# Moving the value products of three attention chunks, spreading weight traffic and adding one output buffer in a fused attention and feed-forward kernel

## The chip, the cores and the metric

The kernel runs on one core of one Trainium2 chip. The metric is the time of one execution on the device in microseconds (us). The core's engines are TensorE (PE, with its weight loads shown apart as PEld), VectorE (DVE), ScalarE (ACT), GpSimd (POOL) and SyncE (SP), which here issues nearly all the DMA transfers. Each engine runs its own instructions in order and waits for the others at semaphores.

## The reference

Eight batches, eight heads, 576 positions, head size 64, in float32. Heads 0 to 3 see a plain window of 32 positions, heads 4 to 7 every fourth position of a window of 128. The attention's output goes through a feed-forward network with an exact gelu.

```python
scores = scale * np.matmul(q, k.transpose(0, 1, 3, 2))
rel = pos[:, None] - pos[None, :]
mask_plain = (rel >= 0) & (rel < window)
mask_dil = (rel >= 0) & (rel < window * dilation) & (rel % dilation == 0)
...
attn = attn / (np.sum(attn, axis=-1, keepdims=True) + 1e-09)
return np.matmul(attn, v).astype(np.float32)
...
x = np.ascontiguousarray(attn_out.transpose(0, 2, 1, 3)).reshape(B * S, H * D)
h = x @ w_in
g = 0.5 * h * (1.0 + erf(h * inv_sqrt2))
return (g @ w_out).astype(np.float32)
```

x is 4608 tokens by 512, w_in 512 by 2048, w_out 2048 by 512.

## The kernel before

**Tiles.** The 4608 tokens are nine chunks of 512: chunks 0 to 7 are the first 512 positions of the eight batches, chunk 8, the last, holds the remaining 64 positions of all of them. Inside a chunk the attention works on four pairs of heads, two plain and two dilated, as blocks of queries against blocks of keys: score products, mask, exp, sums, norm, a transposition, and the *value products* (attention times v), each called a visit here. The feed-forward network works with float32 values split into a high and a low part, and each product is the three products of parts that matter.

**Stage 1, chunk 0 and the attention of chunks 0 and 1.** The order is written out by hand in the string `SCHEDULE`. Each job is a Python generator; a token such as `half0.1.1:a` advances one job by a step on a named engine (a for ACT, d for DVE). The order of the tokens is the order of the instructions on every engine, SP's DMA issues among them. `av0.0` and the like are the value products: `av_wide` (L488) for chunk 0, with v read at 128 rows, `av_early` (L500) for chunk 1. `norm`, `turn` and `half` make what they read: `turn0.3` transposes on TensorE, `half0.x.y` copies it into place. The weights come in as 64-bit words and are split on DVE and ACT (`split`, `rest`, `high`, `join`); `keep0` and so on store a finished weight tile of 1 MB to DRAM (`keep_weight`, L648).

**Stage 2, chunks 1 and 2.** Plain feed-forward: 12 products L603 for a block f of the hidden layer, gelu, then 12 products L626 into the output. Other work is put between by `add(position, rank, job)`: a position counts units of 12 products, with 32 units for each of the two parts of a chunk (positions 32 to 96), and everything due by a position is emitted when the unit is reached. Such work is the attention of later chunks (`whole(2, ...)`, `whole(3, ...)`, `whole(4, ...)`: their scores, softmax, key swaps L379, value products `av_four`, L571, and `x_back`, which give the chunk's x), storing weight tiles 8 to 15, reloading tiles 0 to 7 (`fetch_weight`, L764), and sums of weight tiles (`prepare`) with their stores (`keep_sums`, L804).

**Stage 3, pairs of chunks.** Chunks (3, 4), (5, 6) and (8, 7) go in pairs by seven products of sums in place of eight. A unit of position is one product of 6 multiplications (L1028); a quarter q has 28 products, four quarters a pair. Weights and weight sums come through a ring of tiles from DRAM (`ring_load`, L983). `combine` makes the operands from the chunks' x (L907 on ACT, L912 on DVE), `first_layer` makes the gelu's operands (ACT L1049 stashes a bank in a buffer named u, L1053 copies a bank, L1058 the gelu, L1074 and L1075 the high and low part), `drains` (L1081) adds results from the banks into accumulators on DVE (L1090). The attention of later chunks runs between; for the last chunk's dilated heads (`L23`) the value products are `av_last` (L519) and ACT's copies `x_wide` (L586).

**Buffers.** The pool tag "go" has three buffers, shared in turn by the identity `eye`, the gelu's output `gf`, the output tile `o_sb` before its store, and `u`. A tile takes a buffer when the third tile before it is done with.

## Time and profile before

| | us |
|---|---|
| median of three runs | 890.93 (890.57 to 891.88) |
| profiled execution | 889.42 |
| its span | 887.56 |

The profile shows one execution. Busy time of an engine is the time in which one of its instructions runs; TensorE's mean granted clock over the span is 0.969 of full speed. A row of a timeline joins like instructions that follow each other; the bracket at its end holds the idle time of the engine before them and what ended it. "issue" is idle time in which the engine waited for nothing that the profile shows. A float32 product that isn't split shows as two loads and two products in the trace, so its counts are doubled.

### The profile page before, as it was taken

The page shows a single profiled execution, that of the slowest core. Times are in us where ns is not written, and L with a number is a line of the kernel's source. Part 1 is how long each engine was busy: PE and PEld are TensorE (multiplying, and loading weights), DVE is VectorE, ACT ScalarE, POOL GpSimd, SP SyncE. Part 2 cuts the span into 40 slices and gives each one's busy share as a digit, 9 for nine tenths or more (in the row PEclk, how much of TensorE's full clock was granted, in tenths as well). Part 3 has the DMA queues.
Part 4 walks back from the last instruction along what each step waited for, and adds up shares of the span by engine and source line. Part 5 has one row for each costly group of instructions (what it writes and reads, how often), then busy time and mean ns, then how long its engine had stood idle before and what let it go on. Part 6 is the DMA issues. An engine that isn't in the chain of part 4 may idle for free.

```text
span 887.6 us, 19932 instructions
## 1 busy us (share of the span) xinstructions
PE 827.9 (93%) x8400; PEld 674.6 (76%) x8400; DVE 613.3 (69%) x703; ACT 464.5 (52%) x1081; POOL 95.4 (11%) x92
## 2 busy tenths in 40 slices
PE   7899889998997999899999998997989999999997
PEld 5787768886885877688888876885768777888885
DVE  8697762346675379485959798856538798483977
ACT  7587633543765356473645663744546545243351
POOL 1000002042202430000000026000000045000000
PEclk9999979999998999999999998998899999999999
DMA  9996494932689836877768685966356668566663
GB/s 365 415 419 227 137 421 183 386 104 103 223 313 363 309 125 236 315 246 226 274 202 297 191 310 168 318 225 215 103 165 232 198 205 260 174 205 191 197 198 126
DMA packets 118296, 212.31 MB, mean 239 GB/s; under 512 B 6848, under 2 KB 92864, under 8 KB 110784
## 3 DMA queue, kind: packets, MB, share of 16 engines
q1 hardware_dynamic: 118064, 210.79, 68.1%
q8 instruction: 66, 1.08, 0.5%
q10 hardware_dynamic: 144, 0.26, 0.1%
q14 instruction: 22, 0.18, 0.1%
HBM read 161.21 MB, written 42.99 MB: 230 GB/s over the span
## 4 chain that ended last, share of the span: by engine, by line
PE 77%; DVE 12%; issue 5%; ACT 3%; DMA 2%; SPq 0%; DVEq 0%; ACTq 0%
PE ps L1028 43%; PE ps L603 15%; PE ps L626 13%; PE ps L303 2%; DVE g L1075 2%; PE ps L571 2%; DVE xc L912 2%; DMA raw_w<-w 2%; DVE acc L1090 1%; ACT xn L592 1%; DVE xn L920 1%; DMA outT<-o_sb 1%; PE ps L497 1%; DVE xn L584 1%; PE ps L515 1%
## 5 line engine op out<-in xcount | busy, mean ns | idle before, releaser
L1028 PE MATMUL ps<-xc,ring 128*128 128x512 f32 x1008 | 240.1, 397 | 4.6 <-ACT ps L1053 4.0
L1028 PE MATMUL ps<-g,ring 128*128 128x512 f32 x1008 | 237.4, 395 | 5.5 <-DVE g L1075 2.7
L1028 PEld LDWEIGHTS ps<-g,ring 128*128 128x128 f32 x1008 | 191.2, 191 | 49.4 <-DVE g L1075 5.5
L1028 PEld LDWEIGHTS ps<-xc,ring 128*128 128x128 f32 x1008 | 191.0, 191 | 47.4 <-ACT ps L1053 4.2
L1075 DVE TENSOR_TENSOR g<-g_value,g 128x1024 fp32r<-128x1024 f32 x84 | 103.5, 1241 | 78.9 <-ACT g L1074 78.9
L603 PE MATMUL ps<-x,weight 128*128 128x512 f32 x576 | 142.7, 403 | 1.6 <-issue 1.6
L626 PE MATMUL ps<-g,weight 128*128 128x512 f32 x576 | 136.3, 394 | 1.5 <-issue 1.5
L603 PEld LDWEIGHTS ps<-x,weight 128*128 128x128 f32 x576 | 110.3, 194 | 26.3 <-issue 2.2
L626 PEld LDWEIGHTS ps<-g,weight 128*128 128x128 f32 x576 | 109.3, 190 | 23.3 <-issue 0.2
L1074 ACT CAST g<-g_value 128x1024 fp32r<-128x1024 f32 x84 | 87.1, 1046 | 38.4 <-DVE g_value L1076 21.6
L615 DVE TENSOR_TENSOR g<-gf,g 128x512 fp32r<-128x512 f32 x48 | 35.7, 744 | 76.0 <-ACT g L105 75.9
L1090 DVE TENSOR_TENSOR acc<-ps,acc 128x1024 f32<-128x1024 f32 x56 | 67.6, 1217 | 28.7 <-PE ps L1028 28.7
L1104 POOL TENSOR_TENSOR acc<-acc 128x1024 f32<-128x1024 f32 x14 | 42.1, 3018 | 370.8 <-DVE acc L1090 370.4
L610 ACT ACTIVATE gf<-ps 128x512 f32<-128x512 f32 x48 | 28.7, 598 | 100.9 <-PE ps L603 97.6
L424 ACT ACTIVATE sm<-sm,st 128x64 f32<-128x64 f32 (+1 forms) x224 | 75.4, 339 | 0.2
L780 POOL TENSOR_TENSOR whole<-weight 128x512 f32<-128x512 f32 x32 | 43.8, 1398 | 146.8 <-PE ps L626 54.6
L1049 ACT COPY u<-ps 128x512 f32<-128x512 f32 x48 | 28.2, 588 | 56.4 <-PE ps L1028 29.7
L1053 ACT COPY ps<-ps 128x512 f32<-128x512 f32 x24 | 13.6, 571 | 78.5 <-PE ps L1028 78.5
L424 ACT ACTIVATION_READ_ACCUMULATOR sm<-sm,st 128x1 f32 x224 | 42.1, 188 | 0.0
L912 DVE TENSOR_TENSOR xc<-xn,xc 128x1024 fp32r<-128x1024 f32 x21 | 33.1, 1589 | 11.4 <-ACT xc L907 11.4
L303 PE MATMUL ps<-raw_qk 64*32 64x64 f32 (+1 forms) x2304 | 31.7, 239 | 7.5 <-DVE sm L331 4.3
L303 PEld LDWEIGHTS ps<-raw_qk 64*32 64x32 f32 x2304 | 26.7, 111 | 15.3 <-DVE sm L331 5.1
(123 smaller groups left out, 775.3 us busy)
## 6 DMA issues: line engine op xcount, KB each, us to landing
ring<-sd SPq DMA_DIRECT2D x96, 512.0 KB, 4.6
ring<-wd SPq DMA_DIRECT2D x72, 512.0 KB, 4.5
v_sb<-v SPq DMA_DIRECT2D x17, 1024.0 KB, 9.4
raw_qk<-qk SPq DMA_DIRECT2D x32, 512.0 KB, 7.6
wd<-weight SPq DMA_DIRECT2D x16, 1024.0 KB, 16.7
sd<-sums SPq DMA_DIRECT2D x16, 1024.0 KB, 5.4
raw_w<-w SPq DMA_DIRECT2D x15, 1024.0 KB, 17.4
weight<-wd SPq DMA_DIRECT2D x8, 1024.0 KB, 13.2
```

Of the source, the lines that this page charges most:

```text
L303: nc.tensor.matmul(s.sc[32 * r:32 * r + 32, h, c0:c0 + s.nk], x[:, q0:q0 + 32], x[:, k0:k0 + s.nk], start=s.c > 1, stop=s.c > 1 or u == NU ...
L424: nc.scalar.activation(t, s.sc[:, h, at:at + 2 * KB] if s.c < 2 else t, AF.Exp, bias=st[:, 0], scale=SCALE if s.c < 2 else -1.0, accum_out ...
L603: nc.tensor.matmul(bank, weights[f][:, t, cc * P:(cc + 1) * P], x[:, xx], start=n == 1 and i == 0, stop=n == parts and i == 2)
L615: nc.vector.tensor_sub(g[:, 1], gf, g[:, 0])
L626: nc.tensor.matmul(ps[:, d], weights[f][:, t, DM + d * P:DM + (d + 1) * P], gs[f][:, u], start=f == first and n == 0, stop=f == last and n ...
L780: nc.gpsimd.tensor_add(to, x, y)
L912: nc.vector.tensor_sub(combined[k][:, :, 1], part(*VALUE[k]), combined[k][:, :, 0])
L1028: nc.tensor.matmul(ps[:, bank], lhs, rhs, start=start and i == 0, stop=i == 5, skip_group_check=True)
L1074: add(base + t, 4, run("a", lambda k=k, v=v: nc.scalar.copy(operand(k, 0, final), val(v))))
L1075: add(base + t1, 4, run("d", lambda k=k, v=v: sub(operand(k, 1, final), val(v), operand(k, 0, final))))
L1090: plus(total(m), src, total(m))
L1104: add(base + dt * n, 6, run(e[n], lambda g=g, to=to, x=x, y=y: g.tensor_add(total(to), total(x), total(y))))
```

## The change

- *Chunk 0.* `av_wide` takes both pairs of a kind in one visit, ordered so that four groups of 32 columns follow each other. The tokens `av0.1` and `av0.3` go, `av0.0` moves behind `turn0.3`, and `av0.2` to the place of `av0.3`. The banks of the results are the same.
- *Chunk 1.* `av1.0` and `av1.2` did both pairs in one step; now `av1.0` to `av1.3` are steps of their own.
- *Weight traffic.* `keep0` to `keep7` stand no longer in one run but one by one between other tokens. Tiles 8 to 15 are stored every 1.75 units, not 1.4. The reloads of tiles 0 to 7 start four units earlier and are 2 units apart, not 1.5. The stores of the sums of weights are due a little later.
- *Chunk 2.* Its value products and what follows are due two units later, its x one unit later.
- *First combination.* Operands B11 and B21 of the pair (3, 4) are made some three and two units earlier.
- *Buffers.* The tag "go" gets a fourth buffer.
- *Last chunk.* `av_last` was one run at position 49 into banks 4 to 7. It becomes four visits at 37, 39.5, 46 and 48.5 into banks 6 and 7, each with half of the row blocks for one pair of heads; `x_wide` becomes four copies after each visit, half as wide. The third drain of a quarter is always at 23; before, in this quarter, it was at 20.

The diff, cut to its changed lines and their neighbours:

```diff
@@ -53,22 +53,23 @@
-half0.0.1:a half0.0.0:a turn0.1 sums0.3:d mid2 sums0.3 turn0.2 split1 half0.1.1:a av0.0 norm0.3:d half0.1.0:a split1
-turn0.3 half0.2.0:a av0.1 half0.2.1:a high0.1:d half0.3.1:a rest1 av0.2 w2 qk1.0 half0.3.0:a rest1 x0.0:a av0.3 x0.1:a
+half0.0.1:a half0.0.0:a turn0.1 sums0.3:d mid2 sums0.3 turn0.2 split1 half0.1.1:a norm0.3:d half0.1.0:a split1
+turn0.3 av0.0 half0.2.0:a half0.2.1:a high0.1:d half0.3.1:a rest1 w2 qk1.0 half0.3.0:a rest1 x0.0:a av0.2 x0.1:a
...
-high8:a rest8 qk2.0 av1.0 split9 h7 split9 qk1.3 join10.0 split9 h8 w12 h7:a x1.0:a h7 high9:a x1.0 qk2.1 rest9 o6
+high8:a rest8 qk2.0 av1.0 split9 h7 split9 qk1.3 join10.0 split9 av1.1 h8 w12 h7:a x1.0:a h7 high9:a x1.0 qk2.1 rest9 o6
...
-rest12 turn1.3:a h10 turn1.2:a high12:d join13.1 rest12 av1.2 h11 split13 mid14 h11:a split13 h12 h11 x1.2:a join15.0
-w14 x1.2 split13 o10 x1.3:a h12 x1.3 h12:a rest13 join15.1 h12 o11 rest13 high13:a split14 keep0 keep1 keep2 keep3 keep4 keep5 keep6 keep7 qk2.2 split14*2 h13 qk2.3
-rest14*2 o12 high14:d h13 split15 h13:a split15 h13 h14 split15 rest15*2 o13 high15:a h14 h14:a h15 h14 o14 h15 h15:a
-h15 o15 store0.0:d store0.2:a store0.1:a store0.0 store0.2 store0.3:d store0.3 store0.1
+rest12 turn1.3:a h10 turn1.2:a high12:d join13.1 rest12 av1.2 h11 keep0 split13 mid14 h11:a split13 av1.3 h12 keep1
+h11 x1.2:a join15.0 w14 x1.2 keep2 split13 o10 x1.3:a h12 x1.3 h12:a keep3 rest13 join15.1 h12 o11 rest13 high13:a
+keep4 split14 qk2.2 split14*2 h13 qk2.3 rest14*2 keep5 o12 high14:d h13 split15 h13:a split15 keep6 h13 h14 split15
+rest15*2 o13 high15:a keep7 h14 h14:a h15 h14 o14 h15 h15:a h15 o15 store0.0:d store0.2:a store0.1:a store0.0 store0.2
+store0.3:d store0.3 store0.1
@@ -115,7 +116,7 @@
     turned = early[:, P:2 * P]
-    eye = work.tile([P, P], F32, tag="go", name="eye", bufs=3)
+    eye = work.tile([P, P], F32, tag="go", name="eye", bufs=4)
     ones = const.tile([P, 2 * KB], BF16, name="ones")
@@ -485,16 +486,16 @@
         return [(s.p % 2 * 2 + h, e, slice(h * D + 32 * e, h * D + 32 * e + 32)) for e in range(2) for h in range(2)]
-    def av_wide(s):
+    def av_wide(s, o):
         yield "p"
...
                 c0 = (2 * r + a) * 2 * KB
-                for g, e, cols in parted(s):
-                    t = s.t[:, (2 * (g % 2) + a) * 4 + r]
-                    bank = BANK0[s.p - s.p % 2 + e] + 1
-                    nc.tensor.matmul(ps[32 * g:32 * g + 32, bank, c0:c0 + 2 * KB], s.v[:, a, r, cols],
+                for y, g, e, cols in sorted([(y, *x) for y in (s, o) for x in parted(y)], key=lambda x: (x[2], x[1])):
+                    t = y.t[:, (2 * (g % 2) + a) * 4 + r]
+                    bank = BANK0[s.p + e] + 1
+                    nc.tensor.matmul(ps[32 * g:32 * g + 32, bank, c0:c0 + 2 * KB], y.v[:, a, r, cols],
                                      t.rearrange("p k n -> p (k n)"), start=True, stop=True)
@@ -514,18 +515,16 @@
                         nc.tensor.matmul(to, s.v[rows, a, r, cols], t, start=True, stop=True)
-    WIDE_BANKS = (4, 5, 6, 7)
-
-    def av_last(s, u0):
+    def av_last(s, k):
         yield "p"
-        for u in range(u0, u0 + 2):
+        for u in range(NU):
             for m in range(3):
-                for r in range(4):
+                for r in range(2 * k, 2 * k + 2):
                     rows = slice(32 * r, 32 * r + 32)
                     for h in range(2):
-                        c0 = s.p % 2 * P + u * KB
-                        nc.tensor.matmul(ps[h * D:(h + 1) * D, WIDE_BANKS[r], c0:c0 + KB],
+                        c0 = (2 * k + s.p % 2) * P + u * KB
+                        nc.tensor.matmul(ps[h * D:(h + 1) * D, 6 + r % 2, c0:c0 + KB],
                                          s.v[rows, u, m, h * D:(h + 1) * D], s.t[h][rows, 3 * u + m], start=m == 0, stop=m == 2)
@@ -583,13 +582,13 @@
             nc.vector.transpose(to, src[:, e])
-    def x_wide(s):
-
-        yield "a"
-        c0 = s.p % 2 * P
+    def x_wide(s, k):
+
+        c0 = (2 * k + s.p % 2) * P
         for g, e, cols in parted(s):
+            yield "a"
             to = x_tile(s.c)[32 * g:32 * g + 32, s.p - s.p % 2 + e].rearrange("p (r b i g) -> p r b g i", r=4, b=2, g=4)
-            nc.scalar.copy(to, ps[cols, WIDE_BANKS[0]:WIDE_BANKS[0] + 4, c0:c0 + P].rearrange("p r (b g i) -> p r b g i", b=2, g=4))
+            nc.scalar.copy(to[:, 2 * k:2 * k + 2], ps[cols, 6:8, c0:c0 + P].rearrange("p r (b g i) -> p r b g i", b=2, g=4))
     emitted = {}
@@ -606,7 +605,7 @@
         yield "a"
-        gf = work.tile([P, N], F32, tag="go", name="gf", bufs=3)
+        gf = work.tile([P, N], F32, tag="go", name="gf", bufs=4)
         nc.scalar.activation(gf, bank, AF.Gelu)
@@ -634,7 +633,7 @@
         e = yield "ad"
-        o = work.tile([P, N], F32, tag="go", name="o_sb", bufs=3)
+        o = work.tile([P, N], F32, tag="go", name="o_sb", bufs=4)
         copy(e, o, ps[:, d])
@@ -689,12 +688,14 @@
                 jobs["scores" + k] = scores(s, BANK0[p])
-                jobs["av" + k] = av_wide(s)
+                if p % 2 == 0:
+                    jobs["av" + k] = av_wide(s, xs[c][p + 1])
                 for i in range(2):
...
                 jobs["scores" + k] = one("p", [scores(xs[c][p + i], 6) for i in range(2)])
-                jobs["av" + k] = one("p", [av_early(xs[c][p + i]) for i in range(2)])
+            if c == 1:
+                jobs["av" + k] = av_early(s)
             if c == 0 or p % 2 == 0:
@@ -811,7 +812,7 @@
             add(at + (4.5 + n) * dt, 6, unit_low(s, u, n))
-            add(at + (4.6 + n) * dt, 6, keep_sums(s, u, n))
+            add(at + (6 + n) * dt, 6, keep_sums(s, u, n))
@@ -834,10 +835,12 @@
                 add(base + at["v"] + .1 * n, 0, load_v_wide(o))
-                add(base + at["av"], 6, av_last(o, 0))
-                add(base + at["av"], 6, av_last(o, 2))
-                add(base + at["back"][n], 7, x_wide(o))
-        if not wide:
+        if wide:
+            for k in range(2):
+                for n, o in enumerate(two):
+                    add(base + at["av"][2 * k + n], 6, av_last(o, k))
+                    add(base + at["back"][2 * k + n], 7, x_wide(o, k))
+        else:
             add(base + at["low"], 2, lowest_half(*two))
@@ -858,15 +861,15 @@
             attend(c, i, base, t)
-    whole(2, 32, None, 2, 2, 8.2, 7, 22, 28)
+    whole(2, 32, None, 2, 2, 8.2, 7, 24, 29)
     whole(3, 32, 10, 19.5, 2, 24.2, 29, 36)
...
     for f in range(NF // 2, NF):
-        add(33 + 1.4 * (f - NF // 2), 0, keep_weight(f))
+        add(33 + 1.75 * (f - NF // 2), 0, keep_weight(f))
     for n, u in enumerate((4, 5, 6, 7)):
...
     for f in range(NF // 2):
-        add(32 + 34 + 1.5 * f, 0, fetch_weight(f))
+        add(32 + 30 + 2 * f, 0, fetch_weight(f))
     for n, u in enumerate((0, 1, 2, 3)):
@@ -877,7 +880,7 @@
     H23 = later(H01, QT)
-    L23 = dict(H23, scores=(2, 4.4), low=(2.5, 4.9), av=49, back=(50, 51.5), v=20)
+    L23 = dict(H23, scores=(2, 4.4), low=(2.5, 4.9), av=(37, 39.5, 46, 48.5), back=(41.5, 42.5, 49.5, 50.5), v=20)
     for j in range(NPP - 1):
@@ -927,7 +930,7 @@
     combine(3, 4, {k: [P0 + x for x in t] for k, t in dict(
-        B11=(0, -10, -9.5), B21=(0, -9.4, -8.9), T1=(-8.6, -7.8, -7), B22=(0, -2.4, -1.6), T3=(-6, -4.5, -4), T2=(-6.4, -5.6, -4.8),
+        B11=(0, -13, -12.4), B21=(0, -11.5, -10.9), T1=(-8.6, -7.8, -7), B22=(0, -2.4, -1.6), T3=(-6, -4.5, -4), T2=(-6.4, -5.6, -4.8),
         T4=(-3.5, -3, -2.5)).items()})
@@ -1045,7 +1048,7 @@
             def fn():
-                spare_tile[k, i] = work.tile([P, N], F32, tag="go", name="u", bufs=3)
+                spare_tile[k, i] = work.tile([P, N], F32, tag="go", name="u", bufs=4)
                 nc.scalar.copy(spare_tile[k, i], bank("a", i))
@@ -1078,7 +1081,7 @@
         add(base + at[3], 4, run("d", lambda: g(val("T4"), val("B21"), val(to2))))
-    def drains(base, q, wide):
+    def drains(base, q):
         for n, b in enumerate(OBANKS):
@@ -1088,7 +1091,7 @@
                     plus(total(m), src, total(m))
-            add(base + (16, 18, 20 if wide else 23, 22, 24, 26, 28)[n], 2, run("d", fn))
+            add(base + (16, 18, 23, 22, 24, 26, 28)[n], 2, run("d", fn))
     FINAL = (("M2", "M1", "M2"), ("M6", "M1", "M6"), ("M7", "M6", "M7"), ("M6", "M6", "M5"), ("M5", "M7", "M5"), ("M3", "M6", "M3"), ("M4", "M7", "M4"))
@@ -1148,7 +1151,7 @@
             else:
-                drains(base, q, PAIRS[(j + 1) % NPP][0] == LAST and q == 1)
+                drains(base, q)
         if j < NPP - 1:
```

## Rows read from the trace of the kernel before

**Rows 1.** The page: each engine's busy time, share of the span and instructions; the chain of work that ended last, its shares by engine; the DMA queue of the kind instruction (packets, MB, share of the 16 engines).

```profile
PE 827.9 (93%) x8400; PEld 674.6 (76%) x8400; DVE 613.3 (69%) x703; ACT 464.5 (52%) x1081; POOL 95.4 (11%) x92
...
q8 instruction: 66, 1.08, 0.5%
...
PE 77%; DVE 12%; issue 5%; ACT 3%; DMA 2%; SPq 0%; DVEq 0%; ACTq 0%
```

**Rows 2.** The waits over the whole span, by engine and line and what they waited for: us in total, times, longest. The first two are TensorE's, the last is SP's.

```profile
PE ps L515 <- issue: 8.7, 2, 6.5
...
PE ps L528 <- issue: 5.9, 2, 4.2
...
SPq L767 <- PE ps L626: 11.4, 1, 11.4
```

**Rows 3.** The timeline of chunk 0's value products, from 18 us: start, us, engine, line, operation, tiles, count, and in brackets the idle time before and its releaser. Four rows of TensorE and one of DVE. (In all timelines start and duration are in us.)

```profile
20.86 1.98 PE L497 MATMUL ps<-zeroed,v_sb 128*32 128x64 f32 x64
22.77 0.66 PE L466 MATMUL ps<-early,sm 128*128 128x128 f32 x4
23.36 1.98 PE L497 MATMUL ps<-zeroed,v_sb 128*32 128x64 f32 x68
26.86 3.47 PE L497 MATMUL ps<-zeroed,v_sb 128*32 128x64 f32 x124 [1.52 <-issue]
...
20.95 0.68 DVE L449 TENSOR_TENSOR sm<-sm,st 128x512 f32<-128x512 f32 x1
```

**Rows 4.** Stretches of the span: from:to and length, then the busy time and count of PE, PEld, DVE, ACT and POOL, TensorE's granted clock, the DMA engines' mean busy share and GB/s. The first seven are stretches of small products, the last four stretches at a low granted clock.

```profile
21.06:26.86 5.80, 4.28 (x137) 3.86 (x131) 3.87 (x5) 3.05 (x6) 0.00 (x0) 1.00 1.02 417
26.86:33.05 6.19, 4.59 (x128) 3.98 (x128) 3.46 (x6) 3.50 (x6) 0.00 (x0) 1.00 1.03 419
74.54:78.10 3.56, 1.37 (x151) 1.28 (x138) 1.59 (x2) 1.43 (x2) 0.00 (x0) 1.00 0.81 263
106.59:114.47 7.88, 1.35 (x150) 1.24 (x140) 0.69 (x1) 0.46 (x1) 0.00 (x0) 0.71 0.99 332
276.52:282.94 6.42, 1.81 (x127) 1.32 (x126) 1.19 (x3) 6.41 (x36) 2.47 (x2) 0.82 1.01 424
613.23:618.97 5.74, 1.50 (x155) 1.38 (x143) 0.13 (x1) 0.00 (x0) 0.00 (x0) 0.66 0.54 200
618.97:622.69 3.72, 2.03 (x128) 1.90 (x128) 0.00 (x0) 0.00 (x0) 0.00 (x0) 0.50 0.02 4
109.91:120.14 10.23, 5.67 (x42) 4.54 (x43) 3.03 (x4) 2.02 (x3) 0.00 (x0) 0.50 1.00 405
219.14:222.54 3.40, 3.40 (x88) 2.83 (x76) 2.46 (x6) 0.00 (x0) 0.00 (x0) 0.50 0.02 5
365.91:369.31 3.40, 3.40 (x10) 2.61 (x9) 0.00 (x0) 0.59 (x1) 0.00 (x0) 0.50 0.84 266
615.09:628.73 13.64, 8.07 (x171) 6.71 (x171) 2.36 (x2) 5.23 (x10) 0.00 (x0) 0.50 0.20 63
```

**Rows 5.** The timeline of chunk 1's second value visit, from 104 us: one row of TensorE, one of SP's DMA issues.

```profile
105.69 2.25 PE L515 MATMUL ps<-turned,v_sb 64*32 64x32 f32 x226
...
105.52 9.07 SPq L650 DMA_DIRECT2D wd<-weight  x8
```

**Rows 6.** The timeline of chunk 2's first value visit, from 211 us: one row of TensorE, one of DVE.

```profile
218.36 2.03 PE L571 MATMUL ps<-v_sb,turned 64*32 64x64 f32 x128 [3.37 <-DVE sm L353]
...
217.09 1.21 DVE L353 SCALAR_TENSOR_TENSOR sm<-ps,masks 128x1024 f32<-128x1024 f32 x1
```

**Rows 7.** The timeline around the reloads of weights, 240 to 292 us: two rows of TensorE, two of SP.

```profile
262.98 1.60 PE L571 MATMUL ps<-v_sb,turned 64*32 64x64 f32 x128
...
282.94 0.42 PE L571 MATMUL ps<-v_sb,turned 64*32 64x64 f32 x3 [4.61 <-issue]
...
253.85 6.10 SPq L379 DMA_DIRECT2D turned<-turned  x6
...
268.82 10.01 SPq L767 DMA_DIRECT2D weight<-wd  x5
```

**Rows 8.** The timeline at the end of chunk 2, from 331 us: two rows of TensorE, one of ACT.

```profile
333.88 1.63 PE L571 MATMUL ps<-v_sb,turned 64*32 64x64 f32 x128 [1.43 <-DVE sm L353]
...
364.98 11.43 PE L1028 MATMUL ps<-xc,ring 128*128 128x512 f32 x42 [4.03 <-ACT ps L1053]
...
363.86 0.59 ACT L105 COPY o_sb<-ps 128x512 f32<-128x512 f32 x1 [6.03 <-DMA outT<-o_sb]
```

**Rows 9.** The timeline in the middle of the first pair's products, from 499 us: one row of TensorE, one of ACT.

```profile
517.12 13.70 PE L1028 MATMUL ps<-g,ring 128*128 128x512 f32 x58 [2.21 <-DVE g L1075]
...
502.42 0.59 ACT L1049 COPY u<-ps 128x512 f32<-128x512 f32 x1 [2.08 <-DVE g_value L1057]
```

**Rows 10.** The timeline of the last chunk's value visits, from 600 us: four rows of TensorE, one of ACT.

```profile
600.77 9.68 PE L1028 MATMUL ps<-g,ring 128*128 128x512 f32 x42
...
612.28 2.44 PE L528 MATMUL ps<-turned,v_wide 32*64 32x32 f32 x226 [1.82 <-DVE acc L1090]
618.97 2.04 PE L528 MATMUL ps<-turned,v_wide 32*64 32x32 f32 x128 [4.24 <-issue]
...
633.54 3.01 PE L1028 MATMUL ps<-g,ring 128*128 128x512 f32 x12 [0.60 <-ACT xn L592]
...
623.45 4.32 ACT L592 COPY xn<-ps 32x512 f32<-32x512 f32 x4 [10.95 <-PE ps L528]
```

## The prediction

> **What bounds the kernel now.** I read the page first [rows 1]. TensorE is busy for 93% of the span and holds 77% of the chain that ended last; the next engine, DVE, holds 12%. So whatever shortens the time is either less TensorE work or a hole in TensorE closed. The counts of multiplications don't change with this edit, so I listed the holes by their releaser [rows 2] and then looked up each in the order of time. Three kinds lie where the diff reaches.
>
> The first kind is put down to "issue", which means that nothing in the profile released them. What they share is their place: in both kinds of attention visits TensorE runs a fixed number of small products from one stop to the next, for instance 128 between going on at 618.97 and at 622.69 [rows 4, 10]. The page's queue 8 carries 66 transfers of kind instruction [rows 1]. With 2 × 8400 instructions on TensorE's two sides that is about 256 instructions, 128 loads with 128 products, for each transfer. I read it so: TensorE runs one packet of 256 instructions while the next is fetched, and the next is asked for when the running one is entered. Rows 4 lists such stretches, each from the moment a packet is entered to the moment TensorE goes on behind it (the entry is counted back along the small products, at 9 to 30 ns each, from the stop). The reader is to see two prices. With the DMA engines idle (share 0.02) it takes 3.72 us, and 3.56 in a stretch at a share of 0.81; in the others, at 0.54 to 1.03, it takes 5.74 to 7.88. A packet of large products runs far longer than that, so its fetch is hidden; a packet of 128 small products runs 1.2 to 2.3 us [rows 5, 10], so the rest shows as a stall.
>
> The second kind is a stop on data: DVE's L353 ahead of L571 [rows 6], ACT's L1053 behind a store [rows 8], DVE's chain ahead of L1028 [rows 9], the drain L1090 and ACT's L592 in the last chunk's stretch [rows 10]. The third is the granted clock: after a hole it is 0.50, that is 1.2 of 2.4 GHz, in four stretches of 3.4 to 13.6 us [rows 4]; half of the busy time in these is lost.
>
> **The change part by part** (gain is positive; each with its bounds).
>
> A. Chunk 0's value products. 256 small products stay 256, now two visits of 128. A row with two column groups at work has 68 in 1.98 us, 29 ns each [rows 3]; with four groups I expect about half, between 29 and the 10 ns of L515 [rows 5]. But the stretch goes by packets: entered at 21.06, resumed at 26.86 (5.80), resumed again at 33.05 (6.19) [rows 4]. The visit av0.0 now stands behind turn0.3, which needs the norm at 20.95 + 0.68 = 21.63 on DVE, and takes 0.66 [rows 3]: 22.3. The packet's edge falls about four products into av0.0, so the next packet is asked for at 22.3, not 21.06. With unchanged fetches TensorE goes on at 22.3 + 5.8 + 6.2 = 34.3: **−1.25**. Bounds: −1.9, if the norm's 0.68 is lost once more; +2.6, if the fetch takes 3.56: 22.3 + 3.56 + 4.59 of work in the second packet is 30.5. I take the row of the place itself, whose DMA load (417 GB/s) the change leaves alone.
>
> B. Chunk 1's split visits. Between the new places stand jobs of ACT, DVE and SP and no product, so TensorE's order is what it was: **0**. Bounds: 2.2 either way, the hole of such a visit there (74.54 to 78.10, 3.56 less 1.37 busy [rows 4]).
>
> C. The eight weight stores. SP issues all eight right at the visit L515 [rows 5], and the packet entered at 106.59 takes 7.88 us, the longest of rows 4, with the clock at 0.50 from 109.91 to 120.14. Spread, the first three stores are still around the visit. Other full-load packets take 5.74 to 6.42, so up to 1.5 is to be had; I take **+1.0**. Bounds: 0; and +7.1, if the fetch falls to 3.56 (4.3) and the clock stays up (half of 5.67 busy, 2.8).
>
> D. The later eight stores and the sums' stores, further apart, the third drain at one place for all: **0**. The stores wait for finished data and nothing of TensorE waits for them; the cover is that ring tiles are fetched ahead. Bounds: 1.8 either way, the one stop on a drain [rows 10].
>
> E. Chunk 2's attention two units later. TensorE stood 3.37 before L571 at 218.36, for DVE's L353 of 217.09 [rows 6], the mask of the next chunk's scores, that shares the banks. Two units, 24 products L603 or L626, are some 5.7 us of work now ahead of the visit, more than 3.37: the hole closes, and with it the half clock from 219.14 to 222.54 (3.40 busy, 1.7 lost): **+5.1**. What is late next is chunk 2's x, which its first layer wants; it comes later by those two units. Bounds: 3.0, if that takes back two microseconds; 5.1.
>
> F. The reloads four units earlier and further apart. TensorE stood 4.61 at 282.94, and that packet took 6.42 at 424 GB/s [rows 4, 7]; SP issued five reloads in a row from 268.82 [rows 7], 1 MB each. Of the eight, some four still fall together, since they wait for buffers: the DMA is still full. **+0.3**. Bounds: −3, if a worse packet meets them; +4.5, if it takes 3.56 (2.8) and the clock's 1.7 goes too.
>
> G. The fourth "go" buffer at chunk 2's last store. ACT's copy at 363.86 had waited 6.03 for a store to land, and behind it on ACT stands L1053, for which TensorE stood 4.03 until 364.98; then the clock is 0.50 until 369.31 (3.40 busy, 1.7 lost) [rows 4, 8]. The fourth buffer takes the wait away: 5.7. Against it, B21's two operations go some two units earlier and put an L912 ahead of an L353, for which L571 stood 1.43 already [rows 8]; that hole once more, and some half clock behind it, I put at 2.0: **+3.7**. Bounds 0 (DVE late for all) and 5.7.
>
> H. The fourth buffer for "u". ACT's L1049 at 502.42 waited 2.08 for L1057 to give a buffer back, then L907 for the next operand; TensorE stood 2.21 at 517.12 behind that chain [rows 9]. It ends some 1.6 earlier, and a like place gives a little: **+2.0**. Bounds 0 and 2.5.
>
> I. The last chunk. From the end of the earlier product, 610.46, to that of the 12 at 633.54, 636.4: 25.9 us [rows 10]. In it are 42 products L1028 (as 42 in 9.68 at 600.77) and 384 small ones (226 in 2.44: 96 in 1.04, four times 4.2): 13.9 without holes. So 12.0 lie in the drain's 1.82, the packets' 4.24 and 1.7, ACT's 0.60, and 8.07 busy at half clock [rows 4, 10]. Four visits of 96 bring back less than a packet each; the two of a pair stand only 12 products (2.7 us) apart, so a packet runs some 4.0 us against a fetch of 3.7 to 5.74, on average 1.05 late, twice: 2.1. ACT's 16 copies of half width, taken at 0.64 (between half of 1.08 and all of it [rows 10]), put eight, 5.1 us, ahead of an operand's gelu; allowance 0.5. Drains: nothing, since banks 6 and 7 are not theirs. **+9.4**. Bounds 0.5 and 12.0.
>
> Sum: −1.25 + 1.0 + 5.1 + 0.3 + 3.7 + 2.0 + 9.4 = 20.25. The profiled execution took 889.42 with a span of 887.56: 869.2, span 867.3. The median of the runs is 1.5 above that execution: **870.7 us**.
>
> **The rivals.**
> 1. *Partial.* The fetches meet loads four times in the last chunk (1.7 each, 6.8 for 2.1: −4.7), DVE eats G (−3.7), C gives nothing (−1.0), A its lower bound (−0.65): 10.1 less, 880.8. For it: of six such stretches beside transfers five paid 5.74 and more [rows 4]. Against: E and most of I don't hang on that.
> 2. *The spreading does free the fetch.* C +7.1 for 1.0, F +4.5 for 0.3: 860.4. For it: 7.88 stands right at eight stores. Against: DMA is full there before the stores too.
> 3. *Fetches don't pace the small products.* Then the holes at issue are the visits' own: A gets 256 × 14.5 ns = 3.7, less 1.25, so +2.4, and I loses no 2.1: 865.0. Rows 4 speaks against it, with one count at each stop. The Trainium skill, "Runtime: NRT & Kernel Launch", section "Instruction fetch mechanics", says this: instructions come in blocks of 256 and the cost of crossing a block is mostly hidden. The block size agrees with the trace's 128 and 128, the hidden cost does not: 4.24 and 6.53 us stood open.
> 4. *Slower: a reload blocks SP.* SP once stood 11.4 at L767 for TensorE's L626 [rows 2]. A reload now comes four units earlier, ahead of the swaps L379 of chunk 3 (six issued from 253.85 over 6.1), which the visit L571 at 262.98 wants [rows 7]: 3.0 to spare. If no buffer is free, swaps and the visit are late by the block less 3.0. To be slower it has to eat 20.25: a block of 23 us, or 17 with half clock behind it. Twice the longest seen.
> 5. *No change.* The holes closed reopen elsewhere to the same sum; TensorE has few others of size.
>
> **How the numbers follow.** Chances: the forecast 0.45 (864 to 879), partial 0.18, freed fetches 0.18, rival 3 0.07, no change 0.04, slower 0.08. A difference under 0.2% can't be told from none. Faster: 0.88; same 0.04; slower 0.08. The range 856 to 885 holds the first four cases with a few microseconds around 860 and 881, and leaves out the last two and their tails.
>
> **What would show it.** A: the first L603 behind the visits starts again near 34.3, and stops keep their 128. C: the hole at L515 is 5 to 6.5, the clock still 0.50 behind it. E: no wait of L571 for L353 near 218. F: a hole above 3 near 275. G: no wait of L1053 for a store. H: the 2.21 shrinks below 1. I: four visits of 96, holes of at most 2 in each pair, the stretch some 16.5 us. Wrong it is above all if the packets' edges fall otherwise into the visits, or if ACT's copies hold up the last chunk's operands.

## The result

The changed kernel took 866.45 us (median of four runs, 863.99 to 868.01) against 890.75: a ratio of 0.973, 95% interval 0.970 to 0.976, 24.3 us faster. The forecast was 870.7, a gain of 20.25 in its sum. The profiled execution has a span of 864.1, 23.4 less than before.

The page of the changed kernel, engines and chain:

```profile
PE 819.9 (95%) x8400; PEld 668.8 (77%) x8400; DVE 617.0 (71%) x703; ACT 466.6 (54%) x1089; POOL 99.7 (12%) x92
...
PE 77%; DVE 9%; DMA 6%; ACT 3%; issue 3%; SPq 1%; DVEq 0%; ACTq 0%
```

The products are the same 8400; their busy time is 8 us less than in [rows 1], for the most part because less of it runs at half clock (27.2 busy, not 40.1, which is 6.5 of the 8), and the rest of the gain is holes. The waits of TensorE (us in total, times, longest):

```profile
PE ps L516 <- issue: 6.7, 2, 4.4
PE ps L570 <- issue: 4.6, 1, 4.6
...
PE ps L570 <- DVE sm L354: 2.6, 2, 2.4
...
PE ps L1031 <- DVE g L1078: 0.7, 1, 0.7
```

L516 stands for L515 of before, L570 for L571, L527 for L528, L602 for L603, L625 for L626, L1031 for L1028. The value visits of the last chunk, 5.9 in [rows 2], have no wait for a packet left. Stretches of the changed kernel, with the columns of [rows 4]; all but the last run from one packet's entry to the next:

```profile
22.80:27.93 5.13, 3.13 (x132) 2.81 (x132) 2.11 (x3) 2.17 (x5) 0.00 (x0) 0.82 1.02 414
27.93:34.13 6.20, 4.59 (x128) 4.06 (x128) 3.30 (x6) 3.63 (x7) 0.00 (x0) 0.72 1.02 419
107.66:113.41 5.75, 1.36 (x149) 1.25 (x140) 0.69 (x1) 0.47 (x1) 0.00 (x0) 1.00 0.97 370
271.71:278.29 6.58, 2.01 (x127) 1.49 (x126) 1.79 (x3) 6.56 (x33) 4.31 (x4) 0.92 0.72 301
604.49:609.25 4.76, 4.76 (x144) 3.95 (x136) 3.80 (x4) 4.73 (x12) 0.00 (x0) 1.00 0.93 338
113.39:116.81 3.42, 3.40 (x38) 2.75 (x38) 2.04 (x3) 2.03 (x3) 0.00 (x0) 0.50 1.03 436
```

And TensorE's timeline where the edit reached it:

```profile
21.75 1.09 PE L467 MATMUL ps<-early,sm 128*128 128x128 f32 x4 [0.85 <-DVE sm L450]
22.77 2.86 PE L498 MATMUL ps<-zeroed,v_sb 128*32 128x64 f32 x128
26.95 0.30 PE L498 MATMUL ps<-zeroed,v_sb 128*32 128x64 f32 x3 [1.32 <-ACT zeroed L106]
27.93 3.70 PE L498 MATMUL ps<-zeroed,v_sb 128*32 128x64 f32 x125 [0.68 <-issue]
...
34.13 4.96 PE L602 MATMUL ps<-x,weight 128*128 128x512 f32 x21 [1.60 <-ACT weight L106]
...
113.41 0.67 PE L516 MATMUL ps<-turned,v_sb 64*32 64x32 f32 x31 [4.39 <-issue]
...
216.65 1.75 PE L570 MATMUL ps<-v_sb,turned 64*32 64x64 f32 x128 [0.18 <-DVE sm L354]
...
236.46 3.81 PE L625 MATMUL ps<-g,weight 128*128 128x512 f32 x16 [1.38 <-issue]
...
272.26 1.46 PE L570 MATMUL ps<-v_sb,turned 64*32 64x64 f32 x124
278.29 0.42 PE L570 MATMUL ps<-v_sb,turned 64*32 64x64 f32 x4 [4.57 <-issue]
...
330.73 1.97 PE L570 MATMUL ps<-v_sb,turned 64*32 64x64 f32 x128 [2.43 <-DVE sm L354]
...
500.00 4.49 PE L1031 MATMUL ps<-xc,ring 128*128 128x512 f32 x19 [1.74 <-issue]
...
587.53 1.60 PE L527 MATMUL ps<-turned,v_wide 32*64 32x32 f32 x96
592.00 1.60 PE L527 MATMUL ps<-turned,v_wide 32*64 32x32 f32 x96
...
603.74 1.60 PE L527 MATMUL ps<-turned,v_wide 32*64 32x32 f32 x96 [0.40 <-ACT xn L591]
608.22 1.60 PE L527 MATMUL ps<-turned,v_wide 32*64 32x32 f32 x96
...
634.73 1.65 PE L570 MATMUL ps<-v_sb,turned 64*32 64x64 f32 x128
```

The last row is the visit that was stopped in the kernel before:

```profile
650.37 1.46 PE L571 MATMUL ps<-v_sb,turned 64*32 64x64 f32 x125
655.04 0.30 PE L571 MATMUL ps<-v_sb,turned 64*32 64x64 f32 x3 [3.21 <-issue]
```

Where the time went follows from the start of the same product in both traces (the n-th of its line). Before minus after, so gained so far: −1.3 at the first L602 after chunk 0's visits, −1.1 at chunk 1's second visit, 2.1 behind it, 4.8 behind chunk 2's visits (at 243 of before), 4.1 behind the reloads (288), 1.6 at 337, 7.2 at 369, 4.6 at 505, 6.9 at 517, 15.5 at 634, 20.4 at 659, 23.4 at the end.

| part | forecast | profile |
|---|---|---|
| A and B, chunks 0 and 1 | −1.25 | −1.1 |
| C, first stores | +1.0 | +3.2 |
| E, chunk 2's visits | +5.1 | +2.7 |
| F, reloads | +0.3 | −0.7 |
| G, buffer less early operands | +3.7 | +3.1 |
| a hole of 1.74 at 498, one of 0.59 at 411 | none | −2.6 |
| H, buffer for u | +2.0 | +2.3 |
| I, last chunk | +9.4 | +8.6 |
| the hole at 651 of before | none | +4.9 |
| the rest, 659 to the end | none | +3.0 |

The terms of the forecast brought 18.1 of their 20.25; 5.3 belong to no term. Of the rest, 1.6 is half clock behind a stop of 2.15 at 873 of before; the like stop of the changed kernel, 2.11 at 852, has none behind it.

### The profile page after: what moved, and what is told of

The parts are those of the page before. It is cut to its first block, busy times and chain, and to the rows that moved or that the text cites. A ratio compares the mean times of both kernels' runs of the same rounds, so it can differ in the third digit from the quotient of the medians.

```text
span 864.1 us, 19933 instructions
## 1 busy us (share of the span) xinstructions
PE 819.9 (95%) x8400; PEld 668.8 (77%) x8400; DVE 617.0 (71%) x703; ACT 466.6 (54%) x1089; POOL 99.7 (12%) x92
## 4 chain that ended last, share of the span: by engine, by line
PE 77%; DVE 9%; DMA 6%; ACT 3%; issue 3%; SPq 1%; DVEq 0%; ACTq 0%
PE ps L1031 44%; PE ps L625 13%; PE ps L602 13%; PE ps L304 2%; DMA turned<-turned 2%; PE ps L570 2%; DMA raw_w<-w 2%; DVE g L1078 1%; DMA ring<-wd 1%; DVE acc L1093 1%; DMA v_sb<-v 1%; DVE sums L791 1%; PE ps L498 1%; PE ps L527 1%; PE ps L516 1%
## 5 line engine op out<-in xcount | busy, mean ns | idle before, releaser
L1031 PE MATMUL ps<-xc,ring 128*128 128x512 f32 x1008 | 237.5, 393 | 2.2 <-issue 1.7
L1031 PE MATMUL ps<-g,ring 128*128 128x512 f32 x1008 | 232.9, 390 | 2.8 <-issue 2.1
L1031 PEld LDWEIGHTS ps<-g,ring 128*128 128x128 f32 x1008 | 188.2, 188 | 44.8 <-DVE g L1078 3.1
L1031 PEld LDWEIGHTS ps<-xc,ring 128*128 128x128 f32 x1008 | 188.7, 189 | 43.8 <-ACT g_value L1061 1.9
L602 PE MATMUL ps<-x,weight 128*128 128x512 f32 x576 | 139.7, 397 | 1.6 <-ACT weight L106 1.6
L625 PE MATMUL ps<-g,weight 128*128 128x512 f32 x576 | 138.6, 398 | 2.4 <-issue 2.4
L625 PEld LDWEIGHTS ps<-g,weight 128*128 128x128 f32 x576 | 110.5, 193 | 26.6 <-issue 3.2
L602 PEld LDWEIGHTS ps<-x,weight 128*128 128x128 f32 x576 | 108.7, 191 | 25.4 <-issue 1.8
L781 POOL TENSOR_TENSOR whole<-weight 128x512 f32<-128x512 f32 x32 | 48.0, 1532 | 140.2 <-PE ps L625 38.0
```

What stands on the lines that cost most here:

```text
L602: nc.tensor.matmul(bank, weights[f][:, t, cc * P:(cc + 1) * P], x[:, xx], start=n == 1 and i == 0, stop=n == parts and i == 2)
L625: nc.tensor.matmul(ps[:, d], weights[f][:, t, DM + d * P:DM + (d + 1) * P], gs[f][:, u], start=f == first and n == 0, stop=f == last and n ...
L781: nc.gpsimd.tensor_add(to, x, y)
L1031: nc.tensor.matmul(ps[:, bank], lhs, rhs, start=start and i == 0, stop=i == 5, skip_group_check=True)
```

## The experiments

My theory was that of the forecast: a hole put down to issue is the fetch of a packet of 256 instructions, and the gain is the sum of single holes. Against it stood that the holes belong to the visits, that fetches hang on the number of stores in the queues, and that parts need each other. The experiments ran on two chips (e1 to e8, e9 to e12), where the kernel before had medians of 887.4 (beside e1 to e4), 890.0 (e5 to e8) and 890.1 (e9 to e12) and single runs from 881 to 896. So times are read loosely here, and what is to be told apart is read in the traces, hole by hole.

**Moving every edge between packets** (e1 by half a packet, e2 by a whole one).

```diff
-    BURN = 54
+    BURN = 118   # e1; 182 in e2
```

> The changed kernel (866.45 us) with 64 more of the tiny warm-up products in front, so that every edge between two packets of 128 loads and 128 products falls 64 products earlier in the same order of work. The products themselves take about 1.1 us (54 took 0.93) and lie in the 1.30 us that TensorE waits there anyway. Theory of packets: the holes put down to issue belong to the edges. The visit that is stopped 4.57 at 273.72 is freed, and visits that now lie between two edges (counted in the trace of after: near 321, 386, 480 and 621) are stopped 2 to 3.5 us each. Counting all edges with a fetch of 3.7 us gives 3.5 us more of holes than now, with 5.5 us 15.8, before the half clock behind them: 870 to 885 us. Rival, the holes belong to the visits themselves (their data, their banks): the same holes at the same visits, 866 within 1.5.

> The changed kernel with 128 more of the tiny warm-up products: one whole packet, so that every edge falls again where it fell, one packet later. The 2.2 us of products reach 0.9 beyond the wait that covers them. Theory of packets: holes at issue at the same visits and of the same size as in the changed kernel (4.39 at 109, 4.57 at 274, 1.38 at 235), time 866.45 plus 0 to 1. If e1's time came from the extra products or from the clock at the start and not from the edges, this kernel is slower than e1.

Measured 871.7 and 870.1 (spans of the profiles 872.6 and 866.4). In e1, then in e2, the visits beside the reloads:

```profile
262.90 1.31 PE L570 MATMUL ps<-v_sb,turned 64*32 64x64 f32 x102
268.88 0.66 PE L570 MATMUL ps<-v_sb,turned 64*32 64x64 f32 x26 [4.67 <-issue]
```

```profile
274.10 1.46 PE L570 MATMUL ps<-v_sb,turned 64*32 64x64 f32 x124
280.41 0.42 PE L570 MATMUL ps<-v_sb,turned 64*32 64x64 f32 x4 [4.84 <-issue]
```

A whole packet leaves the stop where it was, after 124 of 128 products. Half a packet takes it away from that visit altogether and stops another one, after 102 products: counting 256 instructions at a time puts the edge there, 103 products in. Nothing of that visit's data had changed. In e1 another visit, at 333.7, is newly stopped, 2.73, and the score products at 155.5, 3.18. Of the four new stops that I had named, near 321, 386, 480 and 621, none came at its place. So the place of an edge is shown to decide where a stop can be; its length isn't told by the place alone. The times don't separate the theories, since e2's is within 2 of e1's; the places do.

The traces hold more than these two runs. I number TensorE's rows (loads, products and the semaphore waits between them) in the order of their start. All 14 traces together have 143 stops put down to issue. Of these, 129 fall on row 193 or 194 of a block of 256, and the other 14 are one of 2.1 near the end of each trace. The stops of more than 1.0 us on those two rows from 20 us on are 104, and every one ends 1.25 to 1.60 us after a transfer of queue 8 has ended. So these stops are waits for packets, in every trace.

**The last chunk alone** (the kernel before with `av_last`, `x_wide`, their positions and the drain at 23 of the changed kernel).

```diff
-    L23 = dict(H23, scores=(2, 4.4), low=(2.5, 4.9), av=49, back=(50, 51.5), v=20)
+    L23 = dict(H23, scores=(2, 4.4), low=(2.5, 4.9), av=(37, 39.5, 46, 48.5), back=(41.5, 42.5, 49.5, 50.5), v=20)
...
-                        nc.tensor.matmul(ps[h * D:(h + 1) * D, WIDE_BANKS[r], c0:c0 + KB],
+                        nc.tensor.matmul(ps[h * D:(h + 1) * D, 6 + r % 2, c0:c0 + KB],
```

> The kernel before with the last chunk's part alone (four visits, banks 6 and 7, the narrower copies, the drain at 23). By the prediction's term I the stretch from 610 to 636 gets 9.4 us shorter: 881.5. By the trace of after it is 9.1. The kernel before had a hole of 3.21 at 651.83 and 1.7 of half clock behind it, which the trace of after doesn't have. If that belongs to this part too: 876.5. If the four visits lean on the other edits (the buffer), less than 6: over 885.

Measured 876.7. The stretch gained 9.0 by the starts of the products on both sides, without any other part. The hole behind it was gone too, which e5 to e12 take up.

**The buffer alone**, and **the changed kernel with B11 and B21 at their old places**.

```diff
-    o = work.tile([P, N], F32, tag="go", name="o_sb", bufs=3)
+    o = work.tile([P, N], F32, tag="go", name="o_sb", bufs=4)   # e4: all four such lines
```

> The kernel before with the fourth go buffer alone. By the prediction's terms G without B21's part (5.7) and H (2.0): 883.2; the hole of 4.03 at 361 and most of the 2.21 at 515 are gone. Rival, another wait takes their place (the trace of after has a new hole at issue of 1.74 near 498): 885 to 888. If the first store's wait only moves to another engine: 889 to 891.

```diff
-        B11=(0, -13, -12.4), B21=(0, -11.5, -10.9), ...
+        B11=(0, -10, -9.5), B21=(0, -9.4, -8.9), ...   # e10
```

> The changed kernel with B11 and B21 made where the kernel before made them. By the prediction's term G the earlier operands cost: the hole ahead of L570 at 328.3 falls from 2.43 to about 1.2 and its half clock goes, 2.3 us gained. Theory from e4: the early operands keep DVE free for the norm and the key swaps of the visit at 369; without them the visit waits for the swaps as in e4 (0.84 and 1.78, some 3.2 with the clock), 2.6 to 3.2 lost. Net by this theory 0 to 1 slower; by the prediction's term alone 2 faster.

e4 measured 883.9, a ratio of 0.997 whose interval (0.993 to 1.000) reaches no gain at all; e10 measured 874.2. The visit at the end of the first products, in e4:

```profile
372.22 0.32 PE L571 MATMUL ps<-v_sb,turned 64*32 64x64 f32 x8
373.38 0.44 PE L571 MATMUL ps<-v_sb,turned 64*32 64x64 f32 x16 [0.84 <-DMA turned<-turned]
375.61 1.25 PE L571 MATMUL ps<-v_sb,turned 64*32 64x64 f32 x104 [1.78 <-DMA turned<-turned]
```

and in e10, with the earlier visit that waits for the mask:

```profile
330.84 1.63 PE L570 MATMUL ps<-v_sb,turned 64*32 64x64 f32 x128 [1.13 <-DVE sm L354]
...
367.62 0.32 PE L570 MATMUL ps<-v_sb,turned 64*32 64x64 f32 x8
368.34 0.44 PE L570 MATMUL ps<-v_sb,turned 64*32 64x64 f32 x16 [0.40 <-DMA turned<-turned]
370.47 1.76 PE L570 MATMUL ps<-v_sb,turned 64*32 64x64 f32 x104 [1.69 <-DMA turned<-turned]
```

By the starts of the products, the buffer alone gains 5.9 at L1028 and gives back 3.4 some 10 us later: the key swaps land late. It gains 2.5 at 517, term H. Making B11 and B21 earlier costs 2.7 ahead of 338 (the hole of 1.13 was 2.39 in e11, and its half clock) and brings 3.7 at 374: e10 is 1.8 ahead of e11 before both places, 4.5 between them and 0.8 behind. Net 1.0 for the early operands by the traces; the times, 874.2 and 875.3, don't tell the two apart. In the prediction they were a pure cost.

**An edge moved by four instructions** (two more warm-up products), in the kernel before and in the changed one.

```diff
-    BURN = 54
+    BURN = 56
```

> The kernel before with two more of the tiny warm-up products: four more instructions on TensorE's two sides, nothing else. In the trace of before two visits L571 have an edge between packets 4 instructions ahead of their first product, 276.84 and 650.37, and these are stopped 4.61 and 3.21; in the trace of after the second of them has it 8 ahead and isn't stopped. Theory: two semaphore waits stand right ahead of a visit, TensorE's sequencer comes to them some 4 us before the visit runs, and an edge behind them is passed only when they open, one ahead of them 4 us earlier. Then both holes go, with half of 6.8 and of 3.4 us at half clock: up to 4.6 + 3.4 + 3.2 + 1.7 = 12.9, at least 6. Rival, the hole at 650 went because of the last chunk's new visits: 890.9 within 1.5 and both holes there.

> The changed kernel with two more of the tiny warm-up products. Its visit at 272.25 has an edge 5 instructions ahead and is stopped 4.57, with the clock at 0.50 for 6.83 from 277.23. Theory as in e5: the edge is now 9 ahead, the hole goes and half of the 6.8: 858.5 to 861.5. Rival, edges don't matter at this size, or the fetch falls into full DMA queues anyway: the hole stays, 866 within 1.5.

Measured 892.1 (one run of 2,048 among ten aside) and 872.1, beside 890.0 for the kernel before. In e5, then in e6:

```profile
284.38 0.43 PE L571 MATMUL ps<-v_sb,turned 64*32 64x64 f32 x5 [4.63 <-issue]
...
655.13 0.31 PE L571 MATMUL ps<-v_sb,turned 64*32 64x64 f32 x5 [0.21 <-issue]
```

```profile
416.51 0.42 PE L570 MATMUL ps<-v_sb,turned 64*32 64x64 f32 x21 [3.12 <-issue]
```

The stop near 650 went, that near 280 stayed in e5 and (4.86) in e6. e6's 872.1 lies above what the theory and its rival gave, and a visit was newly stopped, at 416.51; the other traces of this order stand less than 1 at that visit. e5's time shows no gain (a ratio of 1.003, 1.000 to 1.007). Half a hit, and the runs e11 and e12 undid that half.

**The changed kernel again**, and **chunk 2's attention alone**.

> The changed kernel once more, beside the others, as the kernel that e6 to e10 are to be compared with: 866.45 within 3, holes of 4.4 at 109 and 4.6 at 274.

```diff
-    whole(2, 32, None, 2, 2, 8.2, 7, 22, 28)
+    whole(2, 32, None, 2, 2, 8.2, 7, 24, 29)   # e12, in the kernel before
```

> The kernel before with chunk 2's attention two units later, alone. By term E 5.1 faster (885.8): the hole of 3.37 at 218 and its half clock go. By the trace of after the second of these visits, moved too, now meets an edge beside full DMA queues (a hole at issue of 1.38 near 235): 1.4 to 1.7 given back, net 3.0 to 3.5. Rival, chunk 2's x comes late for its first layer near 248: a wait of L603 for it there, net under 2.

e11 measured 875.3 (874.3 to 877.0), against 890.1 for the kernel before on that chip: a ratio of 0.980, interval 0.978 to 0.983. Its trace is 9.3 us longer than the first one of the same kernel. Half of that, 4.8 with the clock behind it, is one place:

```profile
637.40 1.56 PE L570 MATMUL ps<-v_sb,turned 64*32 64x64 f32 x123
641.93 0.33 PE L570 MATMUL ps<-v_sb,turned 64*32 64x64 f32 x5 [2.96 <-issue]
```

e12, with the order of the kernel before and its edge 4 instructions ahead of that visit, is not stopped there by a packet:

```profile
218.73 1.66 PE L571 MATMUL ps<-v_sb,turned 64*32 64x64 f32 x128 [0.96 <-DVE sm L353]
...
237.50 2.79 PE L626 MATMUL ps<-g,weight 128*128 128x512 f32 x11 [0.24 <-issue]
...
647.76 1.26 PE L571 MATMUL ps<-v_sb,turned 64*32 64x64 f32 x104 [0.56 <-DMA turned<-turned]
```

So the hole of 3 at that visit comes and goes between executions of one program. In the traces of queue 8 it is one of two cases: the packet starts to arrive some 4.2 us ahead of the visit (after, e3, e6 to e9, e2; 3.7 in e12), and nothing stops, or 2.1 behind its start (before, e4, e10, e11), and TensorE stands 3. e5 lies between (1.2 ahead, 0.21). What decides between the two is open. The theory of e5 is refuted: both cases occur with the edge 4 and with the edge 8 instructions ahead.

Chunk 2's part alone has a ratio of 0.994 (0.990 to 0.998) and gained 3.3 by the starts of the products ahead of and behind it (0.6 to 3.9). The first visit brought 3.9, since the hole of 3.37 fell to 0.96, not to nothing; 0.7 went from the packet behind the second visit on, and L603 had no wait for x near 248.

**The first weight stores.**

```diff
-av1.3 h12 keep1
+av1.3 h12          # e7: keep0 to keep2 some tokens later; e9: all eight behind qk2.2
```

> The changed kernel with its first three weight stores later too, so that no store is issued before the second visit of chunk 1 has run; loads of weights stand around the visit as before. Theory, the transfers queued ahead of the packet set its time: the hole of 4.39 at 109 falls to 2 to 3.5 and the time by 1 to 2.5. Rival, the full DMA engines are the weights' loads (405 GB/s behind the visit): the hole stays over 4, the time within 1.

> The changed kernel with all eight first weight stores behind the token qk2.2, whose loads SP can issue only when their buffer is free, near 119 us. In e7 SP had come to the moved stores at 107.16 all the same, so that run didn't hold them back. Now no store is in the queues when the second visit of chunk 1 asks for its packet at 107.7; the loads of weights issued at 104.1 and 106.2 (1 MB each) are. Theory, what is queued ahead sets the fetch: with two loads and no store the packet takes 4 to 5.2 us and the hole at 109 falls from 4.39 to 3 to 3.6. Rival, one full DMA queue is like another: 5.7 or more, the hole over 4.3. Time 864 to 869 for both, since the stores now meet the reads of stage 2.

In e7 SP came to the moved stores at once, at 107.16, right behind the load of 106.79: that run held nothing back, and its hole was 6.57, as the 6.53 of the kernel before. e9 did hold them. First TensorE in the kernel before, then TensorE and SP in e9:

```profile
114.47 0.66 PE L515 MATMUL ps<-turned,v_sb 64*32 64x32 f32 x30 [6.53 <-issue]
```

```profile
114.05 0.67 PE L516 MATMUL ps<-turned,v_sb 64*32 64x32 f32 x31 [6.02 <-issue]
```

```profile
105.24 0.33 SPq L174 DMA_DIRECT2D raw_w<-w  x1
...
123.51 0.90 SPq L649 DMA_DIRECT2D wd<-weight  x2
```

With no store before 123 the stop is 6.02. It is 6.02 to 6.78 in the seven traces where the load of 1 MB comes first (before, e3, e4, e5, e7, e9, e12), and 4.39 to 4.96 in the six where `keep0` had been issued ahead of that load, L174, and the edge lay at the same place (after, e2, e6, e8, e10, e11). The theory of e9 fails: fewer transfers ahead did not shorten the fetch. The rival's numbers hold (over 4.3), but not its reason, since one order of the queue is not like another. Nor is it how busy the DMA engines are as a whole: in e9 their share was 0.18 from 110 to 111, 0.13 from 111 to 112 and 0 from 112 on, and the packet still started only at 111.79, as the last packets of the load ended (111.79 and 111.82). What shortened the fetch goes with the order, a store ahead of the load; why, no run tells. e9's times, 865.1 to 876.9, and e7's, 867.4 to 880.2 (medians 873.8 and 874.8), spread as widely as they do among the executions of the changed kernel.

**Chunk 0's visits as before**, in the changed kernel.

```diff
-    def av_wide(s, o):
+    def av_wide(s):
```

> The changed kernel with chunk 0's value products as in the kernel before: four visits of 64 products, av0.0 ahead of turn0.3. By the prediction's term A and the trace of after, the first large products start again at 33.05, not 34.13: 1.1 to 1.3 us faster, 865.2. Rival, the fuller use of the columns pays elsewhere in the start: 866.5 to 868.

Measured 867.2, the lowest median of this part. Its large products behind the visits are 1.7 earlier than in the changed kernel's first trace; the hole at chunk 1's first visit was then 3.31, not 2.35, and took 1.0 of it back. Over all traces the place bears out term A: these products go on at 34.13 to 34.68 with the new visits (after, e6, e7, e9 to e11) and at 32.60 to 33.34 with the old ones (before, e3 to e5, e8, e12). That it is faster than the changed kernel isn't shown: that one didn't run on the same chip.

## Right or wrong, step by step

The sum came out 3 us short of the profile's 23.4, and the faster result was forecast, but by terms that are partly off and with one large gain that isn't the change's. That the time came so near is in part luck: +4.9, +3.0 and −2.6 are in no term.

A was right in size and by its own steps: turn0.3 waits for the norm, av0.0 starts at 22.77 (forecast 22.3), and two packets of 5.13 and 6.20 lead to 34.13 (34.3). The profile puts the last stop, 1.60, down to ACT's cast, but that ended at 33.59, and the stop falls on row 193 of its block; in e6 and e7 the same stop is put down to issue. Products four groups wide came every 14 ns at full clock (e11, 128 in 1.99) against 26.5 with two groups, about half, as forecast; the 2.86 of the first trace ran for the most part at half clock, 26.7 ns. It made no difference, since packets set the pace. B was right, and so was D as far as it was seen: from 120 to 212 of before the difference stays at 1.9 to 2.1.

C failed in its reason, and its sign, a hole of 5 to 6.5, was missed (4.39). I priced the packet by how much is queued; e9 shows that the stores are not what makes it long. Nor do the two prices of the forecast, told apart by the share of the DMA engines, hold: the packet of e9 took 7.37 at a mean share of 0.46, one in [rows 4] 3.56 at 0.81. The gain of 3.2 (2.1 of hole, and half clock for 3.42, not 10.23) is within the bounds, by another cause.

E was mis-sized: the step "24 products are more than 3.37, so the hole closes" holds, and the changed kernel has only 0.18 left there; by the starts the first visit brought 4.5. The second visit was moved as well, and I priced that at nothing: L625 stands 1.38 at a packet behind it, 1.6 in all. The bound of 3.0 was for x, which wasn't late.

F was right in its stop: the one beside the reloads stayed, 4.02 to 4.9 in every kernel with the reloads spread, 4.6 to 5.7 in the five without. Rival 2 falls with it. The −0.7 is in part what rival 4 named, in small: chunk 3's visit at 258 waits 0.45 for its key swaps, and 0.70 to 2.23 in e2 and e8 to e11, where it waits in none of the five traces with the old reloads. SP's six swaps ahead of it take 8.97, from 246.68, not 6.10; that the earlier reloads are the cause wasn't tried by themselves.

G was right in both of its numbers (5.6 and −2.5 for 5.7 and −2.0), and wrong in what the second one is: it isn't a loss to be borne, it pays for the key swaps. H was right (2.3).

I: 8.6 to 9.0 for 9.4, by two errors that cancel. The 2.1 of packets didn't come, since TensorE was still busy with the large products between two visits, 12 or 18, when they arrived (604.49 to 609.25: 4.76 long, all of it busy). And each visit of 96 takes 1.60, 16.7 ns a product, not the 1.04 of [rows 10]: 2.2 more for the four. A visit now has two of the four row blocks in work; that this is the cause wasn't tried, since with two banks four row blocks would write two to a bank at once. The Trainium skill, "TensorEngine Tiling (Array Packing)", section "Gotcha 1: PSUM Pressure", says that different row tiles can't use one bank at the same time; no run here shows it. ACT's copies were well estimated (0.62 each):

```profile
613.02 2.49 ACT L591 COPY xn<-ps 32x256 f32<-32x256 f32 x4
```

Left out of the sum were the 4.9 at 651 and the −2.6 between 369 and 505. Both are packets for the most part. The first stood in the trace of before and is in no term of the sum; without it the profile's gain is 18.5, and e11 shows 14.8 against its own chip's kernel before. Rival 3 is refuted by e1 and by the rows on which the stops fall: visits are stopped where the edges are put. Rival 1 didn't come: C and G brought gains, and the last chunk had no stop at a packet.

## What to carry to other kernels

Count TensorE's instructions: where 256 of them run in less time than a fetch takes beside the transfers of that moment, a stop of up to 6.8 us (e12) stands at the edge, and adding 128 instructions far ahead of it moved it to other visits (e1). Breaking a long run of small products into pieces with large ones between removes the stop (I); moving it for the sake of data can meet an edge elsewhere (E). Before a gain is put down to an edit, run both kernels again: a hole of 3 us with its half clock, 5 in all, came and went in one and the same program.

## What the runs showed of the hardware

A stop of TensorE at the edge of a packet ended 1.25 to 1.60 us after that packet's transfer on queue 8, which itself took 0.88 to 1.53, in all 104 such stops; what differs is the wait from the entry of the packet ahead to the transfer's start, 1.1 in the stretch with idle DMA engines (618.97 of before), 3.4 to 5.9 at chunk 1's second visit. Behind loads alone a packet took 7.4 us (e9, entered at 106.68, going on at 114.05) at a mean DMA share of 0.46, with a store ahead of the last load 5.75 at a share of 0.97: more traffic, shorter fetch. The Trainium skill, "Runtime: NRT & Kernel Launch", section "Instruction fetch mechanics", calls the cost of a block's edge mostly hidden. It was hidden in the last chunk of the changed kernel (4.76 long, 4.76 busy), and it was not at 109, 4.39. A packet's start on queue 8 fell either some 4 us ahead of a visit or 2.1 behind its start, with one trace of thirteen in between. Small products that use two of four row blocks took 16.7 ns each at full clock, against 10.8 with four; products that fill the rows and use four of four column groups came every 13.9 ns, with two groups every 26.5.
